# FNet mixing with a hard-swish MLP on one core: WN of two steps as products, an order of transfers, and tables that carry their zeros

## The chip, the cores and the metric

The kernel runs on one core of one Trainium2 chip. Its time is the device time of an execution in microseconds, the median of three runs. A profile of one more execution shows what each engine did: PE is the matmul engine (TensorE; PEld its weight loads), DVE is VectorE, ACT is ScalarE, POOL is GpSimd, SP is SyncE. SP only issues transfers here; ACT and POOL issue some beside their work.

## The reference

```python
# x: 8 x 3008 x 256, w_in: 256 x 2048, w_out: 2048 x 256, all float32
X = np.fft.fft(x, axis=1)
X = np.fft.fft(X, axis=2)
y = X.real.astype(np.float32).reshape(24064, 256)
h = y @ w_in
g = h * np.clip(h + 3.0, 0.0, 6.0) / 6.0
out = (g @ w_out).astype(np.float32)
```

## The kernel before

The transform along the sequence is split as 3008 = 47 x 64. The first stage is products with tables of 47 rows (`F`), the second stage products with tables of 64 rows per batch (`T`, six slices, one per group `gr` of four frequencies). The transform along the last axis is folded into w_in: `fold_w_in` multiplies a piece of w_in by the cosine and sine table `C` and writes `W1`. The batches are handled as four pairs; each pair has 12 chunks, and each chunk runs eight steps `fc` through the two MLP products. A step of a chunk is `mlp1_products` (u and v on PE), `activate` (VectorE adds, ACT relu, VectorE gates) and the products with w_out (`mlp2`, or `mlp2_first` in the first chunk).

All of this is steady from about 110 us on. Everything around the change is in the start. There the first pair is handled by halves (one batch at a time), and the first chunk's eight steps are interleaved by hand with the preparation of the weights, since each step needs its own piece of `W1` and `G` (the mixed w_out). The order of instructions on each engine is the order in which the program states them; no scheduler moves them.

The preparation of a weight piece `j` is: `load_w(j)` (a transfer that GpSimd issues), `exponent_a(j)` (ACT writes `PM`), `exponent_b(j)` (PE, `ex`), `exponent_c(j)` (ACT on `ex`), `mantissa(j)` (two VectorE instructions, L785 and L786), and `join(j)` (VectorE multiplies both; into `wi` for w_in, into `G` for w_out). For w_in, `fold_w_in(j)` follows: eight passes on PE (L827), a copy to `W1` (L830 or L834).

One row of the transformed input, the middle frequency, does not fit into the 127 rows that v has. It enters in `activate`: s = qn * WN + u (L566), with `qn` the row spread over all partitions, and `WN` the last row of W1's second block, turned into a column. Before, `send_wn` makes each of WN's 16 columns with a transfer from `W1[127, 1, f*128:(f+1)*128]` to `WN[:, f]` on SP's queue (L815), two after each fold.

First stage of batch 0: four units, in the order `FIRST`, each giving a tile `z`. `evict_first` copies it out of PSUM. Frequency groups 0 and 1 go from `z` to their place in `g` by direct transfers inside SBUF (`turn_first(gr, k)`, two per group and unit, L370); groups 2 and up go through DRAM later. Before, the loop issues both groups' transfers for each unit, and the last ones are placed by hand: one of group 0's last pair on ACT's queue, and group 1's last pair behind `fold_w_in(0)` with its two WN transfers. Group 0's `g` is multiplied by `stage2_half(hb, 0)` (L458) and `spread_by_pe` (L487) into `q` and `qn` for the first chunk; group 1's by a second `stage2_half` (L466) into `spare[0]`, copied to the second half of `q` (L1066).

Both of these take their table from `TF`, which comes with `c_dim`. `T` itself is used by all later second-stage products. For each batch b, 64 of its 128 rows hold the table and the other 64 must hold zeros. Before, `clear_table` writes the zeros with six memsets of 64 x 1024 on GpSimd (L888, at three places in `beside`), and `load_t` brings each slice in two transfers of 128 KB (L840).

SP and ACT share eight completion semaphores, used in turn; a transfer waits until the transfer that used its semaphore before has landed.

Of the kernel before, what the change touches and what calls it, by code (L numbers as in the profile page):

```python
# [7 lines left out]
F32 = mybir.dt.float32  # L8
# [41 lines left out]
N1, N2 = 47, 64  # L50
NK1 = (N1 + 1) // 2
# [7 lines left out]
def kernel(  # L59
# [10 lines left out]
    nc = tc.nc  # L70
    P = nc.NUM_PARTITIONS
# [12 lines left out]
    NM = NXC // 2  # L84
# [117 lines left out]
    def fold_columns(x, part, eng):  # L202
        near, far = x[:, :, 1:P], x[:, :, D - 1:P:-1]
        eng.tensor_tensor(near, near, far, op=AL.add)
        eng.scalar_tensor_tensor(far, far, (-2.0, 2.0)[part], near, op0=AL.mult, op1=(AL.add, AL.subtract)[part])
# [57 lines left out]
    def bank(shape, name):  # L263
        if starting[0]:
            return ps_a.tile(shape, F32, tag="acc", name=name)
        return ps_d.tile(shape, F32, tag="d", name=name)
# [100 lines left out]
    def turn_first(gr, k, last=nc.sync):  # L367
        for u in range(KK):
            to, fr = turns.pop((gr, k, u))
            (last if u else nc.sync).dma_start(out=to, in_=fr)  # L370
# [113 lines left out]
    def spread_by_pe(hb, ps, tab, copy=nc.scalar.copy):  # L484
        row_tile(first, 0)
        for u in range(KK):
            nc.tensor.matmul(ps[:, u * P:(u + 1) * P], hb.g[0][:, u, D:D + 1].to_broadcast([P, P]),  # L487
                             both_tables(0, 1, u, tab), start=True, stop=True)
        copy(first.qn[0][:, 0:TB], ps)
        del hb.g[0]  # L490
# [285 lines left out]
    def exponent_c(j):  # L776
        nc.scalar.activation(exs[j].bitcast(I32), exs[j], AF.Identity, scale=2.0 ** 23)
# [36 lines left out]
    def send_wn(f):  # L814
        nc.sync.dma_start(out=WN[:, f:f + 1], in_=W1[P - 1:P, 1, f * P:(f + 1) * P])  # L815

    def fold_w_in(j):

        _, n, k = PIECES[j]
        nb = WB // 2  # L820
        fc = 2 * n + k
        wi = w.pop(PIECES[j]).rearrange("p (i f) -> p i f", i=2)

        ps = bank([P, 2, nb], "wps") if starting[0] else spare[k]
        for blk in range(2):
            for i in range(2):
                nc.tensor.matmul(ps[:, blk], C[:, i, blk * P:(blk + 1) * P], wi[:, i], start=(i == 0), stop=(i == 1))  # L827
        if j == 1:
            for blk in range(2):
                nc.scalar.copy(W1[:, blk, fc * nb:(fc + 1) * nb], ps[:, blk])  # L830
                if blk == 0:
                    exponent_c(2)
        else:
            (nc.vector.tensor_copy if j == 0 else nc.scalar.copy)(W1[:, :, fc * nb:(fc + 1) * nb], ps[:])  # L834
        for f in range(2 * fc, 2 * fc + 2):
            send_wn(f)

    def load_t(gr, ks=slice(0, 2 * KK), queue=nc.sync):
        for b in range(2):
            queue.dma_start(out=T[b * N2:(b + 1) * N2, b, gr, :, ks], in_=c_stage2[gr, :, :, ks])  # L840


    def load_table():
# [21 lines left out]
    for i in range(2):  # L865
        nc.vector.memset(bias[:, i:i + 1], (2 * i - 1) * 7.5 / 16.0 - 896.0)
    E = FI[:, NIX + 1:].bitcast(F16).rearrange("p (i n) -> p i n", i=2)
    PM = [wpool.tile([P, 2, WB], I16, tag="PM", bufs=3, name="PM") for j in range(3)]

    def clear_bytes(j, eng=nc.vector):  # L870
        eng.memset(PM[j][:].rearrange("p i n -> p (i n)").bitcast(I32), 0x64006400)

# [3 lines left out]
    for k, t in enumerate(units[2:]):  # L876
# [3 lines left out]
        else:  # L880
            nc.scalar.copy(unused.rearrange("p (n d) -> p n d", n=2),
                           Z[PB // 2:PB].unsqueeze(1).to_broadcast([PB // 2, 2, 2 * TB]))

    def clear_table(b, groups, eng=None):
        r = slice((1 - b) * N2, (2 - b) * N2)
        t = T[r, b, groups].rearrange("p g a k n -> p g (a k n)")
        if eng:
            eng.memset(t, 0.0)  # L888
        else:
            nc.scalar.copy(t, Z[r].unsqueeze(1).to_broadcast([N2, groups.stop - groups.start, 2 * TB]))  # L890

    def head(j):
        exponent_a(j)
# [33 lines left out]
        hb.g[gr] = gpool.tile([P, 2 * KK, D + 1], F32, tag="g", name="g")  # L927
    for j in range(1, 3):
        clear_bytes(j, nc.gpsimd)
    fold_columns(zero.unsqueeze(1), 0, nc.vector)  # L930
    exponent_a(0)
    mantissa(0)
# [10 lines left out]
    for k, m in enumerate(FIRST):  # L943
        ps, pt = first_banks(m)
        x, xn = hb.x.pop(m), hb.xr.pop(m)
        unit_columns(m, 0, x, ps)
        if k > 0:
            evict_first(hb, FIRST[k - 1], *before)
            for gr in range(2 if k < NM - 1 else 1):
                turn_first(gr, k - 1)  # L950
        unit_middle(m, 0, x, pt)
        unit_middle(m, 1, xn, pt)
        for j in range(2) if k == NM - 1 else (None,):
            unit_columns(m, 1, xn, ps, j)
        before = ps, pt
    evict_first(hb, m, *before)
    turn_first(0, k, nc.scalar)
    turn_first(1, k - 1)

    seen = wpool.tile([P, 1], F32, tag="seen", name="seen")  # L960
    mantissa(1)
    fold_w_in(0)
    turn_first(1, k)
    exponent_a(1)
    keep_awake(1)
    exponent_b(1)
# [7 lines left out]
    mantissa(2)  # L974
    stage2_half(hb, 0, tab=TF)
    spread_by_pe(hb, bank([P, TB], "ps3")[:], TF)
    exponent_a(2)
    starting[0] = False
    spare = [ps_a.tile([P, 2, WB // 2], F32, tag="acc", name="spare") for h in range(2)]
# [5 lines left out]
    def beside(p):  # L985
        ahead, behind = {}, {}

        def put(t, f, *a, at=ahead):
            at.setdefault(t, []).append((f, a))

        cur = pairs[p]

        if p == 0:
            for gr in range(2, NG):
                put(gr, load_t, gr)
            for gr in range(2):
                put(14 + gr, load_t, gr)
            put(2, spread_half, halves[0], 1)
            for b in range(2):
                put(1, clear_table, b, slice(2, 4), nc.gpsimd)  # L1000
                put(2, clear_table, b, slice(4, NG), nc.gpsimd)
                put(9, clear_table, b, slice(0, 2), nc.gpsimd)
            put(4, load_table)
            put(NF - 1, close_w)
            for i, t in enumerate((3, 5, 7, 8)):
                put(t, mix_w_out, i)
            for gr in range(2, NSG):
                put(8 * gr - 10, load_g_half, halves[0], gr)
                put(8 * gr - 5, stage2_half, halves[0], gr)
                put(8 * gr - 4, spread_half, halves[0], gr)  # L1010

            hb = halves[1]
            put(1, load_zero, zero_slot(hb), hb, nc.sync)
            for k, m in enumerate(ORDER):
                if k > 0:
                    put((5, 8, 11)[k - 1], take_half, hb, m)
                    put((5, 8, 11)[k - 1], load_half, hb, m)
                for part in range(2):
                    put((4, 6, 11, 14)[k] + part, fold_half, hb, m, part, nc.gpsimd)
                put((8, 10, 15, 18)[k], stage1_quarters, hb, m, at=behind)  # L1020
            for gr in range(NSG):
                put(8 * gr + 23, load_g_half, hb, gr)
                put(8 * gr + 27 - (gr == 0), stage2_half, hb, gr)
                put(8 * gr + 28 - (gr == 0), spread_half, hb, gr)

        def s2(t, pr, gr):
            for i in range(2):
                put(t + 3 + 4 * i, stage2, pr, gr, i)
            put(t + 8, spread, pr, gr)

        for gr in range(1 if p > 0 else NSG, NG):
            if gr > 1:
                put(NST * (gr - 2) + 12, load_g, cur, gr)
            s2(NST * (gr - 1), cur, gr)
        if p + 1 < NP:
            nx = pairs[p + 1]
            for c in range(NXC):
                t = 9 * c if p > 0 else 24 + 6 * c
                put(t, load_x, nx, c)
                put(t + 3, fold, nx, c, 0, nc.gpsimd)  # L1040
                put(t + 5, fold, nx, c, 1, nc.gpsimd)
                put(t + 8, stage1, nx, c, at=behind)
            put(NST * (NG - 1) - 2, load_g, nx, 0)
            put(NST * (NG - 1) + 8, load_g, nx, 1)
            s2(NST * (NG - 1), nx, 0)
        return ahead, behind
# [15 lines left out]
    exponent_b(2)  # L1062
    activate(*chunk(0), *uv)
    ps = spare[0]
    stage2_half(halves[0], 1, copy=lambda o, i: None, ps=ps, tab=TF)
    nc.scalar.copy(first.q[0][:, :, TB:], ps[:])  # L1066
    mantissa(3)
    fold_w_in(1)
    join(2)
    exponent_a(3)  # L1070
    head(4)
# [109 lines left out]
def _tables(B, S, D):  # L1181
# [55 lines left out]
    for b in range(2):  # L1237
        rows = t[0:2, :, :, b::2].reshape(2, 2, 2, 4, 2, 2, 2, 2, N2)
        tf[:, b, :, :, :, :, :, :, :, b] = rows.transpose(4, 1, 2, 5, 3, 0, 6, 7, 8)
    d = np.concatenate([d.reshape(2, h, D).swapaxes(0, 1).reshape(h, -1), tf.reshape(h, -1)], axis=1)  # L1240
    return {
        "c_stage1": f.astype(np.float32),
        "c_stage2": t.astype(np.float32),
        "c_dim": d.astype(np.float32),
    }

# [30 lines left out]
```

## Time and profile before

| what | us |
|---|---|
| median of 3 runs (lowest, highest) | 1939.95 (1938.17, 1943.65) |
| the profiled execution | 1939.86 |
| its span | 1938.1 |
| PE busy | 1917.7 |
| VectorE busy | 1432.8 |
| GpSimd busy | 1449.7 |
| ACT busy | 677.4 |

The span begins and ends with the engines' instructions; the execution's time holds it and 1.76 us around it. In a row of the timeline stand the start, the length, the engine, the line, the operation, output<-input with shapes, how many, and in brackets the idle time ahead of it and what ended that. A row of the chain has start, length and what. "SPq" and "ACTq" are issues of transfers on those queues; the transfer itself goes on behind them.

### The profile page before, as it was taken

What the parts mean: (1) busy time and instruction counts of PE and PEld (TensorE: products, weight loads), DVE (VectorE), ACT (ScalarE), POOL (GpSimd) and SP (SyncE); (2) the same over time, 40 slices, a digit from 0 to 9 for tenths busy, and PEclk for the clock granted to TensorE, in tenths of its full rate; (3) what the DMA queues carried; (4) which work ended last, traced back from release to release, by engine and by line L of the source; (5) the groups of instructions that cost most, each with busy time, mean ns of one, the idle gap of its engine ahead of it and who ended that gap; (6) DMA issues with size and microseconds to landing.
All of it is one profiled execution on the core that took longest, in us unless ns stands there. A gap on an engine that the chain in (4) does not pass through costs nothing.

```text
span 1938.1 us, 28339 instructions
## 1 busy us (share of the span) xinstructions
PE 1917.7 (99%) x9398; PEld 1652.8 (85%) x9398; DVE 1432.8 (74%) x2754; ACT 677.4 (35%) x1166; POOL 1449.7 (75%) x1659
## 2 busy tenths in 40 slices
PE   8999999999999999999999999999999999999998
PEld 4578888888988888888898888888899888888888
DVE  7876776777777777777787777777778777777777
ACT  5533333333333333333333333333333333333332
POOL 4587888887678877787678887878667667666765
PEclk9999999999999999999999999999999999999999
DMA  7432122311111222111111221122110101101000
GB/s 252 122 96 55 51 73 69 82 44 32 38 34 50 61 72 55 44 50 32 37 36 47 56 55 44 50 52 53 36 28 20 28 17 26 31 17 28 17 21 20
DMA packets 154905, 98.21 MB, mean 51 GB/s; under 512 B 122319, under 2 KB 136378, under 8 KB 154758
## 3 DMA queue, kind: packets, MB, share of 16 engines
q1 hardware_dynamic: 142206, 57.58, 12.4%
q0 software_dynamic: 11264, 38.20, 6.7%
q8 instruction: 74, 1.21, 0.3%
q10 hardware_dynamic: 1288, 0.62, 0.1%
q14 instruction: 73, 0.60, 0.1%
HBM read 59.87 MB, written 36.79 MB: 50 GB/s over the span
## 4 chain that ended last, share of the span: by engine, by line
PE 95%; DVE 2%; DMA 1%; ACT 1%; issue 0%; ACTq 0%; SPq 0%; DVEq 0%
PE acc L652 56%; PE v L557 16%; PE u L557 16%; PE ps L505 2%; PE ps L277 1%; PE acc L632 1%; DVE a L608 1%; PE spare L827 1%; DVE s L566 0%; ACT t L605 0%; DMA WN<-W 0%; DVE o L713 0%; DMA g<-z 0%; DVE u L589 0%; PE ps L466 0%
## 5 line engine op out<-in xcount | busy, mean ns | idle before, releaser
L622 POOL TENSOR_TENSOR c<-a 128x512 f32<-128x512 f32 (+1 forms) x375 | 469.4, 1252 | 358.3 <-PE acc L652 301.5
L652 PE MATMUL acc<-c,G 128*128 128x256 f32 (+1 forms) x3008 | 697.2, 375 | 0.0
L605 ACT ACTIVATE t<-u,half 128x512 f32<-128x512 f32 (+1 forms) x384 | 260.6, 679 | 1146.3 <-DVE u L576 1067.0
L652 PEld LDWEIGHTS acc<-c,G 128*128 128x128 f32 x3008 | 565.2, 190 | 71.5 <-POOL c L622 0.4
L566 DVE SCALAR_TENSOR_TENSOR s<-qn,WN,u 128x256 f32<-128x256 f32 (+1 forms) x768 | 330.6, 472 | 344.2 <-PE u L557 338.3
L652 PE MATMUL acc<-a,G 128*128 128x256 f32 (+1 forms) x2256 | 541.6, 376 | 0.0
L652 PEld LDWEIGHTS acc<-a,G 128*128 128x128 f32 x2256 | 421.1, 189 | 73.6 <-issue 20.2
L557 PE MATMUL v<-q,W 127*128 127x256 f32 (+1 forms) x1536 | 389.5, 375 | 3.6 <-DVE a L608 3.6
L557 PE MATMUL u<-q,W 128*128 128x256 f32 (+1 forms) x1536 | 388.1, 375 | 0.5 <-ACT W L830 0.5
L608 DVE SCALAR_TENSOR_TENSOR a<-t,u 128x512 f32<-128x512 f32 (+2 forms) x448 | 264.2, 601 | 102.2 <-ACT t L605 97.5
L557 PEld LDWEIGHTS v<-q,W 127*128 127x128 f32 x1536 | 288.1, 190 | 44.0 <-DVE a L608 3.9
L557 PEld LDWEIGHTS u<-q,W 128*128 128x128 f32 x1536 | 285.8, 190 | 38.0 <-issue 2.6
L622 POOL TENSOR_TENSOR c<-a,c 128x256 f32<-128x256 f32 (+1 forms) x375 | 268.5, 716 | 29.4
L622 POOL TENSOR_TENSOR c<-c,a 128x256 f32<-128x256 f32 (+1 forms) x375 | 268.4, 716 | 29.4
L576 DVE TENSOR_TENSOR u<-s,v 128x512 f32<-128x512 f32 x352 | 245.0, 696 | 38.1 <-DVE s L566 1.9
L608 DVE SCALAR_TENSOR_TENSOR a<-t,v 128x512 f32<-128x512 f32 (+1 forms) x480 | 263.7, 566 | 0.3 <-ACT t L605 0.3
L605 ACT ACTIVATE t<-v,half 128x512 f32<-128x512 f32 (+1 forms) x384 | 260.5, 678 | 0.3 <-issue 0.3
L578 DVE TENSOR_TENSOR v<-v,s 128x512 f32<-128x512 f32 x352 | 243.9, 693 | 0.0
L622 POOL TENSOR_TENSOR r<-w,e 128x256 f32<-128x256 f32 (+1 forms) x92 | 88.7, 985 | 3.6
L662 ACT ACTIVATE e<-acc 128x512 f32<-128x512 f32 (+2 forms) x184 | 83.4, 544 | 0.0
L713 DVE STREAM_TRANSPOSE o<-r 128x256 f32<-128x256 f32 (+1 forms) x192 | 72.6, 415 | 0.2
L622 POOL TENSOR_TENSOR w<-w,e 128x512 f32<-128x512 f32 (+1 forms) x46 | 57.5, 1250 | 3.6
(127 smaller groups left out, 786.6 us busy)
## 6 DMA issues: line engine op xcount, KB each, us to landing
out_dram<-o SPq DMA_DIRECT2D x744, 32.0 KB
g<-zd SPq DMA_DIRECT2D x42, 256.0 KB
zd<-z SPq DMA_DIRECT2D x48, 192.0 KB
xt<-in_x_dram POOLq DMA_DIRECT2D x21, 256.0 KB, 3.7
st<-in_moe_w_out_dram POOLq DMA_DIRECT2D x8, 512.0 KB, 6.9
qn<-qd SPq DMA_DIRECT2D x16, 256.0 KB
st<-in_moe_w_in_dram POOLq DMA_DIRECT2D x7, 512.0 KB, 6.1
xt<-in_x_dram POOLq DMA_DIRECT2D x17, 192.0 KB, 4.1
```

The costliest lines, as they stand in the source:

```text
L277: nc.tensor.matmul(ps[b][h * PB:(h + 1) * PB, 0:n], F[rows(b), 0:PB], y[rows(b), 2 * h:2 * h + n], start=True, stop=not last, skip_group_c ...
L505: nc.tensor.matmul(ps[:, blk, u * P:n].rearrange("p (b k) -> p b k", b=2), g[:, kk, blk * (P + 1):blk * (P + 1) + P], T[:, :, gr, blk, kk, ...
L557: nc.tensor.matmul(ps[:, i, 0:nq], W1[r, blk, f * P:(f + 1) * P], q[r, blk, of:of + nq], start=True, stop=True)
L566: nc.vector.scalar_tensor_tensor(s[:, i, 0:nq], qn[:, of:of + nq], WN[:, f:f + 1], u[:, i, 0:nq], op0=AL.mult, op1=AL.add)
L576: nc.vector.tensor_tensor(u[:], s[:], v[:], op=AL.add)
L578: nc.vector.tensor_tensor(v[:], v[:], s[:], op=AL.subtract)
L605: nc.scalar.activation(t, h, AF.Relu, bias=half[:], scale=scale)
L608: nc.vector.scalar_tensor_tensor(dst, t, 1.0, h, op0=AL.min, op1=AL.mult)
L622: (eng or nc.gpsimd).tensor_tensor(out, in0, in1, op=AL.add)
L652: nc.tensor.matmul(ch.acc[i // 2][:, i % 2, 0:ch.n], G[:, i, fc, :], mv, start=(fc == 0 and i % 2 == 0), stop=(fc == NF - 1), skip_group_c ...
L662: nc.scalar.mul(ch.e[:, k:i + 1, 0:ch.n], ch.acc[i // 2][:, 0:i + 1 - k, 0:ch.n], 1.0 / WS)
L713: nc.vector.transpose(o[:, 0:n // DH, h], ch.r[:, m, h, 0:n].rearrange("p (j i) -> p j i", i=DH))
```

## The change

Three things change, all of them in the start or in what it prepares.

- WN of steps 0 and 1 (`fc` 0 and 1, four columns) comes from PE: `wn_by_pe(fc, ps)` multiplies each 128 x 128 block of `W1`'s second block by a unit column (`last_row`, a one in row 127, copied by GpSimd out of the identity that lies in `FI`), and VectorE copies the two results out of PSUM into `WN`. The WN transfers of these two steps go; those of steps 2 to 7 stay. Step 0's products stand behind `spread_by_pe`, step 1's behind the second `stage2_half`. With it, `fold_w_in(1)` moves ahead of that `stage2_half` on PE and its two copies ahead of q's copy on ACT.
- All of group 1's direct transfers are issued behind all of group 0's.
- The host's table `c_stage2` holds the zeros too, each slice with all 128 rows for both batches. `clear_table` goes, and `load_t` brings a slice in one transfer of 512 KB.

```diff
         if j == 1:
             for blk in range(2):
                 nc.scalar.copy(W1[:, blk, fc * nb:(fc + 1) * nb], ps[:, blk])
-                if blk == 0:
-                    exponent_c(2)
+            exponent_c(2)
...
-        for f in range(2 * fc, 2 * fc + 2):
-            send_wn(f)
-
-    def load_t(gr, ks=slice(0, 2 * KK), queue=nc.sync):
-        for b in range(2):
-            queue.dma_start(out=T[b * N2:(b + 1) * N2, b, gr, :, ks], in_=c_stage2[gr, :, :, ks])
+        if j > 1:
+            for f in range(2 * fc, 2 * fc + 2):
+                send_wn(f)
+
+    def wn_by_pe(fc, ps):
+        for i in range(2):
+            f = 2 * fc + i
+            nc.tensor.matmul(ps[:, i:i + 1], W1[:, 1, f * P:(f + 1) * P], last_row[:], start=True, stop=True)
+        nc.vector.tensor_copy(WN[:, 2 * fc:2 * fc + 2], ps)
+
+    def load_t(gr):
+        nc.sync.dma_start(out=T[:, :, gr].rearrange("p b a k n -> p b (a k n)"), in_=c_stage2[gr])
...
+    last_row = wpool.tile([P, 1], F32, tag="last_row", name="last_row")
...
-    def clear_table(b, groups, eng=None):
...
+    nc.gpsimd.tensor_copy(last_row[:], E[:, 0, P - 1:P])
...
             evict_first(hb, FIRST[k - 1], *before)
-            for gr in range(2 if k < NM - 1 else 1):
-                turn_first(gr, k - 1)
+            turn_first(0, k - 1)
...
     turn_first(0, k, nc.scalar)
-    turn_first(1, k - 1)
+    for i in range(NM):
+        turn_first(1, i)
...
     fold_w_in(0)
-    turn_first(1, k)
...
     spread_by_pe(hb, bank([P, TB], "ps3")[:], TF)
+    wn_by_pe(0, ps_d.tile([P, 2], F32, tag="d", name="wn")[:])
...
-            for b in range(2):
-                put(1, clear_table, b, slice(2, 4), nc.gpsimd)
-                put(2, clear_table, b, slice(4, NG), nc.gpsimd)
-                put(9, clear_table, b, slice(0, 2), nc.gpsimd)
...
     ps = spare[0]
+    fold_w_in(1)
     stage2_half(halves[0], 1, copy=lambda o, i: None, ps=ps, tab=TF)
     nc.scalar.copy(first.q[0][:, :, TB:], ps[:])
+    wn_by_pe(1, spare[1][:, 0, 0:2])
     mantissa(3)
-    fold_w_in(1)
     join(2)
```

More of the change, by code (lines that the diff above doesn't have):

```diff
@@ L882 @@
                            Z[PB // 2:PB].unsqueeze(1).to_broadcast([PB // 2, 2, 2 * TB]))
-    def clear_table(b, groups, eng=None):
[L885 to L890, printed above, removed]
     def head(j):
@@ L1239, in _tables @@
         tf[:, b, :, :, :, :, :, :, :, b] = rows.transpose(4, 1, 2, 5, 3, 0, 6, 7, 8)
+    ts = np.zeros((NK1 // 4, 2, N2, 2, 2, 4, N2))
+    for b in range(2):
+        ts[:, b, :, b] = t
     d = np.concatenate([d.reshape(2, h, D).swapaxes(0, 1).reshape(h, -1), tf.reshape(h, -1)], axis=1)
@@ L1242, in _tables @@
         "c_stage1": f.astype(np.float32),
-        "c_stage2": t.astype(np.float32),
+        "c_stage2": ts.reshape(NK1 // 4, 2 * N2, 2, -1).astype(np.float32),
         "c_dim": d.astype(np.float32),
```

## The prediction

> **What bounds the kernel now.** I read the page first: the span, the engines' shares and the chain that ended last.
>
> ```profile
> span 1938.1 us, 28339 instructions
> PE 1917.7 (99%) x9398; PEld 1652.8 (85%) x9398; DVE 1432.8 (74%) x2754; ACT 677.4 (35%) x1166; POOL 1449.7 (75%) x1659
> PE 95%; DVE 2%; DMA 1%; ACT 1%; issue 0%; ACTq 0%; SPq 0%; DVEq 0%
> ```
>
> PE carries 95% of the chain, and nothing that the change touches alters PE's steady work. What can be won lies in the other 5%, nearly all of it in the first 110 us. So I read the chain in order of time there (start, length, what).
>
> ```profile
> 14.67 6.95 DMA g<-z
> 21.72 1.18 ACTq L370
> 23.00 1.41 ACT PM L762 x2
> 24.44 0.38 PE ex L774
> 24.82 0.97 PE ps L458 x8
> 26.25 1.13 PE u L557 x4
> 29.57 1.74 PE spare L827 x8
> 33.10 7.08 DMA WN<-W
> 43.13 3.78 PE spare L827 x8
> 47.77 2.50 PE spare L827 x8
> 93.37 3.44 PE acc L632 x8
> ```
>
> Two transfers stand in the chain: a g<-z that ACT waits for, and the transfer that turns a row of W1 into a column of WN. The timeline shows the second one's price: VectorE waits 4.74 us for it, and PE stands still for 3.96 us behind it. Then I asked for the stretches (PE, PEld, DVE, ACT, POOL busy, granted clock, DMA share, GB/s).
>
> ```profile
> 38.94 0.48 DVE L566 SCALAR_TENSOR_TENSOR s<-qn,WN,u 128x256 f32<-128x256 f32 x1 [4.74 <-DMA WN<-W]
> 43.13 3.35 PE L827 MATMUL spare<-wi,C 128*128 128x256 f32 x7 [3.96 <-DVE wi L794]
> 40.00:42.00 2.00, 0.00 (x0) 0.00 (x0) 1.29 (x3) 0.07 (x1) 0.00 (x0) 1.00 1.03 403
> 44.00:46.00 2.00, 2.00 (x6) 1.53 (x6) 1.86 (x4) 1.02 (x2) 0.11 (x1) 0.50 0.00 0
> ```
>
> The stop costs twice: after it the granted clock is 0.50. The same eight products of L827 take 3.78 and 2.50 us there against 1.74 at 29.57. That is 2.0 + 0.8 us, and with the two ex products between them, about 3.2 us of slow PE behind 4 us of idle PE.
>
> **Part 1: the second group's transfers behind the first's.** In the order of the change, SP issues group 0's transfers for each z as it comes, and group 1's eight only behind all of them. ACT issues one of group 0's last two. Transfers of SP and ACT share eight completion semaphores in turn, and each waits for its semaphore's former user. ACT's transfer closes a row of twelve such transfers before and waits for one of the first four, which lands at 14.67 + 6.95 = 21.62. In the changed order it closes a row of eight, and its semaphore's former user is a constant's load from the start. So it waits only for z, which VectorE finishes last:
>
> ```profile
> 19.73 0.69 DVE L353 COPY z<-ps 128x512 f32<-128x512 f32 x1
> 22.20 0.59 SPq L370 DMA_DIRECT2D g<-z  x1
> ```
>
> That z is done at 20.42. The issue is then 20.46 to 21.64 at the same 1.18 us, the PM pair ends at 23.1 instead of 24.4, and the ex and group-0 products behind it follow: **-1.25 us**. Bounds: 0 if group 0's last transfers land later than 23.4; -1.8 if the issue takes the 0.6 us of most others. They should land in time: before, SP's last one of group 0 is the issue of 22.20 in the fence, over at 22.8, and the products begin at 24.82 without a wait for it, so it takes under 2 us.
>
> Group 1's eight issues follow at about 0.62 us each from 21.1, so the last ends near 26.1 (26.7 before, where two WN transfers stood in between). The cover for this delay is the fold of W1's second step, which now comes ahead of group 1's products on PE: 1.74 us.
>
> **Part 2: WN of steps 0 and 1 by products.** Each wn_by_pe is two f32 matmuls with one moving column, four weight loads in all. Eight passes of 128 columns at L458 take 0.97 us, 0.12 each. No row shows 128-wide weights with a single moving column. If the load sets the pace, four passes take 0.45 us; if the moving side does, nearly nothing. I take 0.45, since those passes are load and product in equal parts, and keep 0.1 to 0.5. VectorE's copy of 128x2 out of PSUM: between the 0.06 us of a tiny instruction and 0.2; I take 0.15. GpSimd's copy of the unit column is one tiny instruction beside its waits: nothing. The four WN transfers removed free 2.4 us of SP's queue, which nobody waits for.
>
> Step 0 did not wait for WN; its s had waited 0.27 us for PE:
>
> ```profile
> 27.49 0.87 DVE L566 SCALAR_TENSOR_TENSOR s<-qn,WN,u 128x256 f32<-128x256 f32 x2 [0.27 <-PE u L557]
> ```
>
> So there the product only costs, **+0.45 us**, since u waits behind it on PE. With part 1, step 0 runs 0.8 us earlier.
>
> Step 1. ACT's order is now: t, t, both W1 copies, ex, then q.
>
> ```profile
> 30.44 0.58 ACT L1066 COPY q<-spare 128x512 f32<-128x512 f32 x1
> 31.33 0.37 ACT L830 COPY W<-spare 128x256 f32<-128x256 f32 x1 [0.31 <-PE spare L827]
> 31.60 0.59 ACT L777 ACTIVATE ex<-ex 128x512 int32<-128x512 f32 x1
> 31.76 1.13 PE L557 MATMUL u<-q,W 128*128 128x256 f32 x4 [0.46 <-ACT W L830]
> 36.37 1.07 ACT L777 ACTIVATE ex<-ex 128x512 int32<-128x512 f32 x2 [1.25 <-PE ex L774]
> 37.34 1.40 ACT L762 ACTIVATE PM<-st,bias 128x512 uint8<-128x512 int16 x2
> ```
>
> q began at 30.44 behind t; with the 0.85 us lead the first W1 copy begins at 29.6. The steps between starts here (0.27, 0.27, 0.52, then 0.6 for q) put q's end at 31.25 and u at 31.3, against 31.76. The second wn_by_pe (30.4 to 30.85) lies inside that wait of PE: nothing. The WN transfer is gone, so what is late next? VectorE could start s at 34.1: behind WN's copy at 31.1 stand two mantissa pairs (1.15 each) and a join (0.7). PE, from u at 31.3: u 0.86, v 0.86, acc 1.72, four ex products 0.86, to 35.6. ACT: two ex 1.07 and the PM pair 1.40, to 38.15; only then t, and VectorE's gate of step 1 at 38.95 instead of 42.99. So the stall of 4.74 us is not won whole; ACT's queue becomes the limit: **-4.05 us** there, parts 1 and 2 together.
>
> Behind it VectorE works almost without gap, except in two places:
>
> ```profile
> 44.19 0.42 DVE L785 TENSOR_SCALAR top<-st 128x512 int32<-128x512 int32 x1
> 46.67 2.12 POOL L888 MEMSET T<- 64x1024 f32 x2
> 46.71 1.19 DVE L785 TENSOR_SCALAR top<-st 128x512 int32<-128x512 int32 x1
> 53.06 0.75 DVE L800 TENSOR_TENSOR G<-top,spare 128x256 f32<-128x256 f32 x2 [1.45 <-ACT spare L777]
> ```
>
> The 1.45 us is a wait for an ex that PE made late at half clock. Without the stop PE keeps its clock, does the first fold from 38.6 to 40.3, and is 6.5 us ahead by then: the wait goes, **-1.45 us**. **Part 3** starts here: the memsets of T on GpSimd go, and the mask instruction that ran beside one (1.19 us against 0.42) gets its 0.77 us back: **-0.8 us**. Sum at 53 us: -4.05 - 1.45 - 0.8 = -6.3 us, PE's lead (-6.5) just above it, so VectorE sets it.
>
> On the clock: the Trainium skill (TensorE: Matmul & The Clock Gate, on why this matters for kernels) says that PE idle beyond some 3 us between bursts brings half rate back. The first stop agrees (3.96 us, then 0.50). The next one does not quite:
>
> ```profile
> 75.88 1.50 PE L557 MATMUL v<-q,W 127*128 127x256 f32 x4 [2.79 <-DVE a L608]
> 77.38 4.76 PE acc L632 x8
> 76.00:78.00 2.00, 2.00 (x5) 1.28 (x6) 2.00 (x5) 2.00 (x4) 1.64 (x6) 0.62 0.31 46
> ```
>
> 2.79 us were enough here. So I count a stop of 2.8 us with its clock loss (v 0.64 and acc 4.76 - 3.44 = 1.32 longer, 1.96 us); by the page's 3 us alone this stop would be free of it, and nothing of it could be won.
>
> **Part 3, the rest.** That stop is VectorE's: its mask and fraction instructions run slowly while GpSimd mixes G and folds x.
>
> ```profile
> 59.92 1.95 POOL L888 MEMSET T<- 64x1024 f32 x2
> 68.00 1.04 DVE L785 TENSOR_SCALAR top<-st 128x512 int32<-128x512 int32 x1
> 69.07 1.10 DVE L786 SCALAR_TENSOR_TENSOR top<-st,top 128x512 f32<-128x512 uint32 x1
> ```
>
> Without the 1.95 us of memset ahead of it, GpSimd's work is done 2 us sooner against VectorE's order, so the last slow pair (1.04 and 1.10 against 0.42 and 0.69) may run free: **-1.0 us**. Bounds: 0, if GpSimd's work meets other instructions as slow; -4, if the stop falls by 2 us and its clock loss goes too. I take -1.0. The third pair of memsets, on GpSimd in the steady part, lies beside products that PE has anyway: 0.
>
> Each T slice now brings its zeros: 512 KB in one transfer instead of 256 KB in two. At 403 GB/s, 256 KB are 0.65 us, for each of six slices, four of them during the start. The products of the start read TF, not T, and SP saves an issue per slice. What stands behind the first slice on SP is the qd and qn pair and the WN transfers of steps 4 and 5:
>
> ```profile
> 65.12 2.47 SPq L815 DMA_DIRECT2D WN<-W  x4
> ```
>
> They are used just ahead of the stop at 73, 5 us after the last issue, and they wait for ACT's W1 copy as much as for the slice. I price the slices at nothing; 0.65 us if that margin is gone.
>
> **The sum.** 1939.86 us is the profiled execution's own time (1.8 us outside its span), 0.1 from the median 1939.95. -6.3 - 1.0 = -7.3: **1932.6 us**. 0.3% is 5.8 us, about what a measurement of this kernel can tell from no change.
>
> **Rivals.**
>
> *The second stop goes as well.* If VectorE gains 2 us before 72 us, PE waits under 1 us and keeps its clock: -6.3 - 2 - 1.96 = -10.3, 1929.6 us. For it: the slow pairs stand just ahead of the stop. Against: GpSimd has as much other work.
>
> *The early lead is lost.* If group 0 lands late or ACT's issue is no earlier, -1.25 falls out, and the last -1.0 may: -5.05, 1934.8 us, within the bound. For it: four short waits in a row must all follow.
>
> *Group 1 lands late; slower.* Now ACT's q copy and VectorE's WN copy both stand behind group 1's products, with four PM and two mantissa pairs queued behind them, so lateness counts one for one. GpSimd's weight loads are issued at 25.2 instead of 26.5, and under their load a transfer took 7.08 us:
>
> ```profile
> 26.49 0.72 POOL L755 DMA_DIRECT2D st<-in_moe_w_out_dram  x1
> 28.00:29.00 1.00, 1.00 (x9) 0.77 (x7) 0.90 (x2) 0.00 (x0) 1.00 (x2) 1.00 0.83 147
> ```
>
> The loads' data move 1.5 us behind the first issue (DMA share 0.83 from 28), so from 26.7 in the changed kernel, when group 1's last transfer has just been issued. It is needed at 29.6. It decides from there: landing at 33 (7 us, as WN's did), PE stops 3.6 us and drops its clock, and only 0.5 to 1 us is left of the gain, 1939 us. Behind the whole backlog, which drains near 42, it would land about 40: u of step 1 at 41.5, ten later than before, the gate at 49.2, +6.2 us: 1946 us. Against it: only one load is ahead of it in any order. The Trainium skill (DMA: Bandwidth & Descriptors, on queues and rings) says that each DMA engine takes turns between queues; by that the wait would be under a microsecond. The 7.08 us of WN's 512 bytes disagree, so I keep the chance.
>
> **How the numbers follow.** Forecast 0.40; second stop gone 0.20; early lead lost 0.22; group 1 late but not slower 0.10; slower 0.08. Faster by over 0.3%: 0.60; within it 0.32; slower by over it 0.08. The range leaves out the last two cases: from 1929.0 (the second stop with its bound) to 1937.0 (the lead lost and half of one more term).
>
> **What would show it.** Right: ACT's L370 issue near 20.5; u of step 1 near 31.3; s without a wait for a DMA; the gate of step 1 near 39, behind ACT's PM; clock 1.00 from 42 to 50; G<-top,spare at about 46.7 without a wait. Wrong: PE waiting at L466 for g, a granted clock below 1 before 60, or everything up to 75 early by 6 us and the lead given back later, which none of these terms allows.

## The result and the profile after

| | median us | lowest, highest | span of the profiled execution |
|---|---|---|---|
| before (6 runs) | 1940.58 | 1938.17, 1943.65 | 1938.1 |
| after (6 runs) | 1931.52 | 1929.91, 1935.19 | 1929.2 |

The ratio is 0.9954, with an interval of 0.9941 to 0.9967: about 9 us faster, where 7.3 were forecast. The profiled spans differ by 8.9 us. The page of the kernel after, the three parts that were shown of before:

```profile
span 1929.2 us, 28340 instructions
PE 1914.9 (99%) x9406; PEld 1652.3 (86%) x9406; DVE 1429.9 (74%) x2756; ACT 677.7 (35%) x1166; POOL 1444.9 (75%) x1654
PE 95%; DVE 2%; ACT 1%; POOL 1%; DMA 0%; issue 0%; ACTq 0%; DVEq 0%; SPq 0%; POOLq 0%
```

PE's share of the chain is the same 95%. The 1% of DMA is gone. Everything that was won lies ahead of the first product of the second half (L381). That product starts at 105.68 before and at 96.66 after, 9.02 us earlier, and what remains of the span behind it is 1832.4 and 1832.5 us. The timeline of before has two rows that the start of after is compared with, the gate of step 1 and that product:

```profile
42.99 0.68 DVE L608 SCALAR_TENSOR_TENSOR a<-t,u 128x512 f32<-128x512 f32 x1
105.68 1.08 PE L381 MATMUL ps<-y,F 47*64 47x512 f32 x8
```

The timeline of after, from the last z to the gate of step 1:

```profile
20.19 0.69 DVE L353 COPY z<-ps 128x512 f32<-128x512 f32 x1 [0.69 <-PE ps L342]
20.96 1.43 ACTq L370 DMA_DIRECT2D g<-z  x1
22.49 1.39 ACT L762 ACTIVATE PM<-st,bias 128x512 uint8<-128x512 int16 x2 [1.85 <-DMA g<-z]
24.25 1.13 PE L458 MATMUL ps<-TF,g 128*128 128x128 f32 x8
26.63 0.15 DVE L842 COPY WN<-wn 128x2 f32<-128x2 f32 x1
30.00 1.30 PE L466 MATMUL spare<-TF,g 128*128 128x128 f32 x8
31.50 1.11 PE L557 MATMUL u<-q,W 128*128 128x256 f32 x4
34.72 0.86 DVE L566 SCALAR_TENSOR_TENSOR s<-qn,WN,u 128x256 f32<-128x256 f32 x2
37.21 1.40 ACT L762 ACTIVATE PM<-st,bias 128x512 uint8<-128x512 int16 x2
39.22 0.69 DVE L608 SCALAR_TENSOR_TENSOR a<-t,u 128x512 f32<-128x512 f32 x1 [1.65 <-ACT t L605]
```

ACT's issue now follows z by 0.08 us (before, z ended at 20.42 and the issue came at 21.72). s of step 1 has no wait in brackets, where 4.74 us for the WN transfer stood. The gate waits for ACT, as forecast; ACT's PM pair ends at 38.61 (forecast 38.15, with a z that came 0.46 later).

Where the two stops stood, the timeline of after has:

```profile
38.88 1.89 PE L827 MATMUL spare<-wi,C 128*128 128x256 f32 x8
42.41 1.99 PE L827 MATMUL spare<-wi,C 128*128 128x256 f32 x8 [0.40 <-DVE wi L794]
47.21 0.75 DVE L800 TENSOR_TENSOR G<-top,spare 128x256 f32<-128x256 f32 x2
67.94 1.13 PE L557 MATMUL v<-q,W 127*128 127x256 f32 x4 [0.70 <-DVE a L608]
```

The stretches there (PE, PEld, DVE, ACT, POOL busy, granted clock, DMA share, GB/s):

```profile
44.00:46.00 2.00, 2.00 (x7) 0.90 (x7) 1.86 (x6) 0.59 (x1) 0.00 (x0) 1.00 0.66 217
70.00:72.00 2.00, 2.00 (x6) 0.84 (x5) 1.82 (x4) 0.78 (x2) 1.72 (x5) 1.00 0.32 48
```

And the chain, the step behind v and the transfer that the end of this section speaks of:

```profile
69.07 3.44 PE acc L632 x8
75.99 4.42 DMA WN<-W
```

The fold that stood 3.96 us for wi now starts at 38.88 without such a wait (the next one waits 0.40 us), and the clock stays at 1.00; G<-top,spare starts at 47.21 without its wait of 1.45. The stop of 2.79 us ahead of v is 0.70, its clock loss is gone too, and acc takes 3.44 us instead of 4.76.

A new wait stands behind it, for the WN transfer of step 6 (the chain's 75.99). The timeline's rows:

```profile
80.44 0.48 DVE L566 SCALAR_TENSOR_TENSOR s<-qn,WN,u 128x256 f32<-128x256 f32 x1 [0.51 <-DMA WN<-W]
96.66 1.08 PE L381 MATMUL ps<-y,F 47*64 47x512 f32 x8
```

### The profile page after: what moved, and what is told of

It is laid out like the page before. It is cut to its first block, busy times and chain, and to the rows that moved or that the text cites. A ratio compares the mean times of both kernels' runs of the same rounds, so it can differ in the third digit from the quotient of the medians.

```text
span 1929.2 us, 28340 instructions
## 1 busy us (share of the span) xinstructions
PE 1914.9 (99%) x9406; PEld 1652.3 (86%) x9406; DVE 1429.9 (74%) x2756; ACT 677.7 (35%) x1166; POOL 1444.9 (75%) x1654
## 4 chain that ended last, share of the span: by engine, by line
PE 95%; DVE 2%; ACT 1%; POOL 1%; DMA 0%; issue 0%; ACTq 0%; DVEq 0%; SPq 0%; POOLq 0%
PE acc L652 56%; PE v L557 16%; PE u L557 16%; PE ps L505 2%; PE ps L277 1%; PE acc L632 1%; DVE a L608 1%; PE ps L342 0%; ACT t L605 0%; DVE s L566 0%; PE spare L827 0%; POOL c L622 0%; DVE o L713 0%; ACT PM L762 0%; PE ps L466 0%
```

## The experiments

The theory was the prediction's account, with the second stop now counted in. WN by products removes the first stop. The memsets on GpSimd make the second one, by slowing VectorE's mask and fraction instructions. The order pays only with the other parts. The rivals were that the clock loss carries most of the gain, that the order does nothing, and that the second stop goes because the start is faster. Each kernel was timed side by side with the kernel before: eleven executions in the first table, five or six in the others. A time "to L381" is the start of that product in the profile, before 105.68.

### Each part alone

WN by products, with the fold ahead; order and tables as before:

```diff
-        for f in range(2 * fc, 2 * fc + 2):
-            send_wn(f)
+        if j > 1:
+            for f in range(2 * fc, 2 * fc + 2):
+                send_wn(f)
...
+    wn_by_pe(0, ps_d.tile([P, 2], F32, tag="d", name="wn")[:])
...
+    fold_w_in(1)
...
+    wn_by_pe(1, spare[1][:, 0, 0:2])
...
-    fold_w_in(1)
```

> Only the products for WN of steps 0 and 1, with the fold of step 1 moved ahead as in the change; transfers and memsets as before. Theory (the first stop and its slow clock are the products' work, the second stop hangs on GpSimd's memsets): the first stop goes, G<-top,spare of step 1 begins about 5.0 us earlier than 53.06, but PE still waits some 2.8 us for a of step 4 and drops its clock there; total about -5 us against before. Rival (the second stop goes by itself once the first is gone, the memsets play no part): about -9 us.

The tables with their zeros, without `clear_table`; the rest as before:

```diff
-        for b in range(2):
-            queue.dma_start(out=T[b * N2:(b + 1) * N2, b, gr, :, ks], in_=c_stage2[gr, :, :, ks])
...
+        nc.sync.dma_start(out=T[:, :, gr].rearrange("p b a k n -> p b (a k n)"), in_=c_stage2[gr])
...
-            for b in range(2):
-                put(1, clear_table, b, slice(2, 4), nc.gpsimd)
-                put(2, clear_table, b, slice(4, NG), nc.gpsimd)
-                put(9, clear_table, b, slice(0, 2), nc.gpsimd)
```

> Only the table slices with their zeros, no memsets; WN and the group transfers as before. Theory: the first stop of 4 us and its half clock stay as they are, VectorE is about 2 us ahead by the second stop, PE waits under 1 us there and keeps its clock: 2.1 + 1.7, about -3.8 us. Rival (the memsets play no part, 1.5 MB more of transfers cost something): 0 to +1 us.

The order of the transfers; the rest as before:

```diff
-            for gr in range(2 if k < NM - 1 else 1):
-                turn_first(gr, k - 1)
+            turn_first(0, k - 1)
...
-    turn_first(1, k - 1)
+    for i in range(NM):
+        turn_first(1, i)
...
     fold_w_in(0)
-    turn_first(1, k)
```

> Only group 1's transfers behind all of group 0's; WN by transfers for all steps, the fold of step 1 where it was. Theory: WN of step 0 now stands behind group 1's eight issues and lands about 1 us after it is wanted, and group 1's products come ahead of the fold and wait about 2 us for their last transfers; the group-0 products start only 0.4 us earlier: +1 to +2 us. By the prediction's own first term (a lead of 1.25 us that is passed on): -1 us.

Nothing of the change, but nine more products in PE's first stop, whose results are not used:

```diff
+            for i in range(9):
+                nc.tensor.matmul(spare[0][:, 0], ones[:], W1[:, 0, 0:TB], start=True, stop=True)
```

> The kernel before, with nine products of 0.43 us on PE whose result nobody reads, put where PE waits for wi behind the WN transfer (39.2 to 43.1). The wait of VectorE for WN stays; only PE's idleness goes. Theory (the stop costs twice, by idling and by the clock behind it): the clock stays 1.00 from 42 to 50, the folds take 1.74 us instead of 3.78 and 2.50, G<-top,spare no longer waits its 1.45 us for the ex, and the time falls by about 1.5 us; more than that cannot come, since VectorE sets the pace behind. Rival (PE's clock loss is hidden behind VectorE anyway): 0.

| kernel | median us (before: 1940.95) | ratio [interval] | to L381 |
|---|---|---|---|
| products only | 1937.38 | 0.9979 [0.9970, 0.9988] | 101.73 |
| tables only | 1937.22 | 0.9982 [0.9973, 0.9991] | 102.25 |
| order only | 1941.82 | 1.0009 [1.0000, 1.0018] | 107.60 |
| PE kept busy | 1940.20 | 0.9997 [0.9988, 1.0006] | 104.98 |

The profile of the products alone begins late: its last z is ready at 22.36, against 20.42 before. So its time to L381 understates what it wins. From the end of the last z to L381 it takes 79.37 us with the products only and 81.28 with the tables only, against 85.26 before and 75.78 after.

The timeline at the second stop, of the kernel with the products only:

```profile
71.92 1.47 PE L557 MATMUL v<-q,W 127*128 127x256 f32 x4 [2.79 <-DVE a L608]
```

The stretch:

```profile
72.00:74.00 2.00, 2.00 (x5) 1.30 (x6) 2.00 (x4) 2.00 (x4) 1.65 (x7) 0.64 0.31 46
```

And of the kernel with the tables only, from the first stop on:

```profile
44.58 3.26 PE L827 MATMUL spare<-wi,C 128*128 128x256 f32 x8 [3.95 <-DVE wi L794]
73.96 1.13 PE L557 MATMUL v<-q,W 127*128 127x256 f32 x4 [0.71 <-DVE a L608]
85.64 0.87 DVE L566 SCALAR_TENSOR_TENSOR s<-qn,WN,u 128x256 f32<-128x256 f32 x2 [1.34 <-DMA WN<-W]
```

The stretch:

```profile
74.00:76.00 2.00, 2.00 (x7) 1.39 (x8) 2.00 (x4) 2.00 (x4) 1.93 (x5) 1.00 0.70 245
```

The two parts take one stop each. With the products the first stop is gone and the second is still 2.79 us, clock loss included. With the tables the first is still 3.95 us and the second is 0.71, at a clock of 1.00. So the second stop hangs on GpSimd's memsets, not on how early the start is done. The wait for WN of step 6 appears here with the tables (1.34 us).

The order alone won nothing. The timeline of that kernel has SP's issues, PE's wait within group 1's products, and VectorE's s of step 0:

```profile
26.71 12.76 SPq L815 DMA_DIRECT2D WN<-W  x4
30.56 0.89 PE L466 MATMUL spare<-TF,g 128*128 128x128 f32 x4 [2.04 <-issue]
31.90 0.48 DVE L566 SCALAR_TENSOR_TENSOR s<-qn,WN,u 128x256 f32<-128x256 f32 x1 [5.39 <-DMA WN<-W]
```

The WN transfers of steps 0 and 1 now stand behind group 1's eight on the same queue, and step 0, which did not wait for WN before, waits 5.39 us, where about 1 us was expected. PE waits 2.04 us between the two halves of group 1's products, about what was expected. The order needs WN by products.

With PE kept busy the first stop's clock loss goes, and VectorE's wait stays; its timeline:

```profile
40.20 0.48 DVE L566 SCALAR_TENSOR_TENSOR s<-qn,WN,u 128x256 f32<-128x256 f32 x1 [5.34 <-DMA WN<-W]
```

The stretch:

```profile
44.00:46.00 2.00, 1.60 (x7) 1.44 (x8) 1.97 (x5) 2.00 (x4) 0.00 (x0) 1.00 0.02 4
```

The clock is 1.00, and the product at L381 comes 0.70 us earlier, or 1.36 us counted from L458, which starts 0.66 us later in this profile. The time's interval holds no change and allows 2.3 us. So by the profile the first stop's clock loss carries about a microsecond, which the times don't tell from nothing; most of the stop's price is VectorE's wait itself.

### One part taken back

The change with the memsets and the half slices as before:

```diff
-        nc.sync.dma_start(out=T[:, :, gr].rearrange("p b a k n -> p b (a k n)"), in_=c_stage2[gr])
+        for b in range(2):
+            queue.dma_start(out=T[b * N2:(b + 1) * N2, b, gr, :, ks], in_=c_stage2[gr, :, :, ks])
...
+            for b in range(2):
+                put(1, clear_table, b, slice(2, 4), nc.gpsimd)
+                put(2, clear_table, b, slice(4, NG), nc.gpsimd)
+                put(9, clear_table, b, slice(0, 2), nc.gpsimd)
```

> The change with the memsets and the half slices of before put back: products for WN and the order of the group transfers alone. Theory (the second stop hangs on the memsets): PE waits 2.8 us for a of step 4, drops its clock, total -4.5 us against before. Rival (the second stop is only an echo of the first): -9 us.

The change with both groups' transfers issued unit by unit as before:

```diff
-            turn_first(0, k - 1)
+            for gr in range(2 if k < NM - 1 else 1):
+                turn_first(gr, k - 1)
...
-    for i in range(NM):
-        turn_first(1, i)
+    turn_first(1, k - 1)
...
     fold_w_in(0)
+    turn_first(1, k)
```

> The change with both groups' transfers issued together for each unit, as before. Theory (the order's lead is 0.4 us at the group-0 products, and 0.2 to 0.3 us of it goes again in waiting for group 1): the same as the whole change within 1 us, -8 to -9 us. By the prediction's first term (-1.25 us, passed on whole): -7.8 us.

| kernel | median us (before: 1940.93) | ratio [interval] | to L381 |
|---|---|---|---|
| without tables | 1934.86 | 0.9965 [0.9952, 0.9979] | 100.95 |
| without order | 1933.49 | 0.9964 [0.9952, 0.9976] | 98.96 |

Without the tables the stop is back. The timeline of that kernel:

```profile
55.54 1.95 POOL L895 MEMSET T<- 64x1024 f32 x2
71.13 1.13 PE L557 MATMUL v<-q,W 127*128 127x256 f32 x4 [2.79 <-DVE a L608]
```

The stretch:

```profile
72.00:74.00 2.00, 2.00 (x5) 0.93 (x4) 1.90 (x5) 1.32 (x2) 1.64 (x4) 0.56 0.30 46
```

The time alone (6 to 7 us faster than before) lies between what the two theories gave; the rows decide. What the tables are worth in the whole change is 2.1 us by the ratios, whose intervals overlap, and 4.3 in the profiles to L381 (of which 0.84 is a wait of PE at L466 in this profile). The five times of this kernel spread from 1932.43 to 1935.81, and the profiled one, 1935.38, is among the slower; so the stop itself is shown, its price in the time only roughly.

Without the order the ACT issue is late again, and the timeline at the start reads:

```profile
22.94 1.18 ACTq L370 DMA_DIRECT2D g<-z  x1
25.02 0.38 PE L774 MATMUL ex<-PM,FI 128*128 128x512 f16 x1 [1.91 <-ACT PM L762]
26.05 1.91 PE L458 MATMUL ps<-TF,g 128*128 128x128 f32 x8
```

The stretch:

```profile
26.00:28.00 2.00, 2.00 (x11) 2.00 (x11) 1.06 (x3) 0.96 (x3) 0.34 (x2) 0.50 0.18 48
```

z was ready at 21.09 here, and the issue came 1.85 us behind it (0.08 in after). PE waits 1.91 us and its clock drops. I had expected the order to be worth at most 0.4 us, reading it from the one profile of after; the medians differ by 2.0 and the ratios by 0.0010, and from the end of the last z to L381 it takes 77.87 us here, 2.09 more than after. The intervals overlap, so its size is not settled. The direction is that of the forecast's first term, 1.25.

### Moving what is left

The change with four slices of T loaded at steps 2, 9, 12 and 13 instead of 2 to 5, run twice:

```diff
-                put(gr, load_t, gr)
+                put((2, 9, 12, 13)[gr - 2], load_t, gr)
```

> The whole change, with the last three table slices loaded at steps 9, 12 and 13 instead of 3, 4 and 5, out of the way of WN's transfers. Theory (behind the two stops the next wait is WN of step 6, 0.51 us on VectorE and 0.37 on PE): that wait goes, -0.4 us against the whole change, about -9.4 us against before; no wait for WN at s of step 6 in the trace. Rival (the slices are hidden): -9.0 us.

> The change with the late slices once more, on the same chip as the changed kernel: 0.7 us less than the changed kernel by its first trace (96.00 - 20.96 against 96.66 - 20.88 from the last z to the first product of the second half), which is near what a measurement can tell.

The change with half slices, and all six memsets later, where PE was thought to cover them:

```diff
-        nc.sync.dma_start(out=T[:, :, gr].rearrange("p b a k n -> p b (a k n)"), in_=c_stage2[gr])
+        for b in range(2):
+            queue.dma_start(out=T[b * N2:(b + 1) * N2, b, gr, :, ks], in_=c_stage2[gr, :, :, ks])
...
+            for b in range(2):
+                put(8, clear_table, b, slice(2, 4), nc.gpsimd)
+                put(9, clear_table, b, slice(4, NG), nc.gpsimd)
+                put(9, clear_table, b, slice(0, 2), nc.gpsimd)
```

> The whole change, but with zeros written by GpSimd after all, all six memsets at steps 8 and 9, and the half slices of before. Theory (what counts is that GpSimd's queue is free between 45 and 65 us, not where the zeros come from): the second stop stays short, -9 us. Rival (the memsets delay GpSimd's c just as the steady products begin, which wait for it): 2 to 6 us of it are lost.

The later slices, and GpSimd's first fold of the second half one step later, run twice:

```diff
-                put(gr, load_t, gr)
+                put((2, 9, 12, 13)[gr - 2], load_t, gr)
...
-                    put((4, 6, 11, 14)[k] + part, fold_half, hb, m, part, nc.gpsimd)
+                    put((5, 6, 11, 14)[k] + part * (k > 0), fold_half, hb, m, part, nc.gpsimd)
```

> The change with the late slices, and GpSimd's first fold of the second half moved from step 4 to step 5, behind its wait for PE. Theory (VectorE's mask and fraction instructions are slow only while GpSimd works beside them): the pairs of pieces 10 and 11, 0.87 + 1.24 + 0.87 in the changed kernel, fall to 0.42 + 0.69 + 0.42, and PE's last 0.7 us of waiting for a of step 4 goes: 0.7 us less than with the late slices alone. Rival (GpSimd's later folds then meet later pairs, or hold the gathers back): nothing, or 1 us lost.

> The late slices and the later fold once more, for a profile in which the first gathers of x land as in the others (there the last z was ready at 25.7 instead of 20.3 to 21.5 us). Theory: from the first group-0 product to the first product of the second half 70.6 us as there, against 71.7 to 72.4 with the change and with late slices; span about 1928, time -10 us against before. Rival (the 70.6 us came from the late start, which gave the weights time to arrive): 71.7 us, -9 us.

The change itself, beside them:

> The changed kernel itself once more, beside the two versions built on it: -9 us against before, as on its first measurement.

| kernel | median us (before) | ratio [interval] | to L381 |
|---|---|---|---|
| slices later | 1931.23 (1940.93) | 0.9961 [0.9947, 0.9974] | 96.00 |
| slices later, again | 1932.26 (1941.31) | 0.9956 [0.9942, 0.9969] | 96.76 |
| zeros late | 1932.66 (1940.93) | 0.9964 [0.9951, 0.9978] | 96.50 |
| folds later | 1930.69 (1941.31) | 0.9947 [0.9933, 0.9961] | 100.59 |
| folds later, again | 1929.38 (1940.79) | 0.9942 [0.9928, 0.9956] | 96.81 |
| the change again | 1931.31 (1941.31) | 0.9951 [0.9937, 0.9964] | 96.31 |

Moving the slices takes step 6's wait for WN away in all four runs that have it, and with half slices at the old steps (zeros late) it does not come either: so the slices of 512 KB at these steps bring that wait. They don't always: without the order they stood there too, and step 6 did not wait. The wait is 0.51 us in one profile of the change and 0.22 in the other. From v of step 4 to L381 these two take 28.72 and 28.43 us, and both runs with the slices later 28.12. The times don't resolve it: the expected 0.4 us is not seen in them (0.9961 and 0.9956, against 0.9954 and 0.9951 of the change).

With the zeros late the second stop stays short (0.70), as the theory has it, and 1.9 us are lost later, as the rival has it: the span behind L381 is 1834.4 us instead of 1832.5. The timeline of GpSimd there shows four memsets between instructions that make `c`:

```profile
104.94 0.73 POOL L622 TENSOR_TENSOR c<-a,c 128x256 f32<-128x256 f32 x1
105.72 3.73 POOL L895 MEMSET T<- 64x1024 f32 x4
109.42 1.27 POOL L622 TENSOR_TENSOR c<-a 128x512 f32<-128x512 f32 x1
```

GpSimd's work on the steady path is delayed by 3.73 us there. That this is where the 1.9 us go was not tried by itself.

With the fold later PE no longer waits at the second stop at all in either run. In the change that fold (L216 and L217) begins at 57.16, beside two pairs of VectorE's mask and fraction instructions. In the second run it begins at 68.82, and the first three instructions of these pairs are:

```profile
59.28 0.60 DVE L785 TENSOR_SCALAR top<-st 128x512 int32<-128x512 int32 x1
59.91 0.69 DVE L786 SCALAR_TENSOR_TENSOR top<-st,top 128x512 f32<-128x512 uint32 x1
61.38 0.42 DVE L785 TENSOR_SCALAR top<-st 128x512 int32<-128x512 int32 x1
```

In after they took 0.87, 1.24 and 0.87 us; here they take 0.60, 0.69 and 0.42, as the theory has it but for 0.18 us of the first. The second run is the fastest kernel measured, 0.9942 against 0.9951 of the change, but the intervals overlap. From the first group-0 product to L381 it took 72.37 us, more than either expectation had (70.6 and 71.7). In that profile PE lost 1.12 us at the start:

```profile
32.11 0.68 PE L466 MATMUL spare<-TF,g 128*128 128x128 f32 x4 [1.12 <-issue]
```

So both runs of that version come out no slower than the change; that it beats it is not shown.

## Why the prediction was right

The range held the time, and 1932.6 lies 1.1 us above the median. Part of that closeness is luck: the forecast starts from one execution of before, 1939.86, which lies 0.7 us below the median of its six. The change won 9.1 us by the medians where 7.3 were forecast. What happened, then, is the rival *the second stop goes as well* (1929.6), less what other terms fell short of it. Step by step, from the profiles:

| step | forecast | measured |
|---|---|---|
| part 1, to the end of the PM pair | -1.25 | -0.97 counted from z's end (the issue took 1.43 us instead of 1.18), -0.5 counted from the start of the span, since z came 0.46 later |
| WN of step 0 by products | 0.45 on PE | 0.34 in the chain |
| VectorE's copy of WN | 0.15 | 0.15 |
| gate of step 1 | -4.05, behind ACT's PM | -3.77, behind ACT's PM |
| G<-top,spare at 53 us | -6.3 | -5.85 |
| the rest of part 3, VectorE | -1.0 | -2.1 to the second stop |
| the same stop's clock loss | 0 | -1.7 |
| slices of T | 0 | +0.6 behind WN of step 6 |
| sum | -7.3 | -9.05 |

The first four rows lie within the fifth, and the sum counts from the fifth on. Counted from z's end, the gate of step 1 is 4.23 us earlier and G<-top,spare 6.31, as forecast (4.05 and 6.3). The signs that the prediction named for being right came in: s of step 1 waits for no DMA, its gate waits for ACT, the clock is 1.00 from 42 to 50, and G<-top,spare has no wait. So the prediction's mechanism held up to 53 us, and what it missed lies behind.

The measured terms from 53 us on are differences of starts: v goes from 75.88 to 67.94 (-7.94, so 2.1 more than the 5.85), and acc's end from 82.14 to 72.51 (-9.63, another 1.7).

**The mis-sized term** is part 3's rest. The prediction freed one slow pair of mask and fraction instructions. The timeline of after shows VectorE's and GpSimd's rows ahead of the second stop:

```profile
57.56 0.87 DVE L785 TENSOR_SCALAR top<-st 128x512 int32<-128x512 int32 x1
58.47 1.24 DVE L786 SCALAR_TENSOR_TENSOR top<-st,top 128x512 f32<-128x512 uint32 x1
61.99 0.42 DVE L785 TENSOR_SCALAR top<-st 128x512 int32<-128x512 int32 x1
62.44 0.69 DVE L786 SCALAR_TENSOR_TENSOR top<-st,top 128x512 f32<-128x512 uint32 x1
64.80 0.73 POOL L810 TENSOR_TENSOR G<-G 128x256 f32<-128x256 f32 x1 [3.74 <-PE acc L632]
```

GpSimd runs out of work at 61.1 and stands until 64.80. The two pairs of VectorE in that time (61.99 to 64.9) run at 0.42 and 0.69 us each, against 0.87 and 1.24 for a pair beside a busy GpSimd. Over the four pairs ahead of the stop that is 5.89 us instead of 7.94, which is the 2.1 us. The kernel with the fold later bears this out: with GpSimd's fold moved away the slow pairs run nearly free. The argument against the rival, that GpSimd has as much other work, failed: GpSimd was not behind any more, but ahead, waiting for PE. The Trainium skill (GPSIMD Engine Reference, key points) says that GpSimd shares its SBUF interfaces with VectorE, with contention for VectorE instructions that run in a 2-port mode or have two SBUF inputs. These rows agree for L786, which reads `st` and `top`; whether L785 runs in such a mode no run here shows.

**The slices** were priced at nothing because of a margin of 5 us at steps 4 and 5. Those steps did not wait. Step 6, which the prediction did not look at, did. The price named for a lost margin, 0.65 us, is near the 0.61 of this profile by chance: in the change's second profile it is 0.31.

**The rivals.** *The early lead is lost* did not happen. *Group 1 lands late* was only grazed: L466's eight passes took 1.30 us in after (1.05 in the change's second profile). PE waited 0.84 us ahead of the second half of them without the tables, and 1.12 us in the second run with the folds later; the profile names no releaser for these two waits. The stop that the prediction reckoned with was 3.6 us.

## What to carry to other kernels

A transfer in a chain of short steps can be replaced by a small product when PE stands still there anyway: four one-column passes at 0.34 us took the place of a transfer of 7.08. Before an idle engine's work is priced at nothing, ask which other engine's instructions run beside it: memsets of 1.95 us on GpSimd shifted its later work onto VectorE's, and cost 3.8 us, by the profiles, at a stop 13 us later; the times show less, 2.1 us without the tables and 3.5 with the tables only, with wide intervals. Parts of a change can depend on each other: the order alone made step 0 wait 5.39 us for WN, a wait that the products take away.

## What the runs showed of the hardware

PE's granted clock dropped after shorter waits than 3 us. Waits of 0.70 to 1.14 us left it at 1.00 (0.70 in after, 1.12 above, 1.14 before at 23.80). After every stop of 2.79 us it was 0.50 to 0.56 in the slowest two-microsecond stretch behind it (before, products only, order only, PE kept busy, without tables). It also fell to 0.50 after 1.91 us without the order, after 2.04 us with the order only, and after 1.43 us at the start of the products only. The 1.60 us ahead of the very first product left it at 1.00. The timeline and a stretch of the products only:

```profile
20.89 0.71 PE L342 MATMUL ps<-xt,F 47*64 47x129 f32 x13 [1.43 <-issue]
22.00:24.00 2.00, 2.00 (x6) 1.55 (x6) 1.39 (x3) 0.21 (x1) 0.00 (x0) 0.50 0.21 63
```

The stretch behind the wait of 2.04 us with the order only:

```profile
32.00:34.00 2.00, 2.00 (x6) 1.55 (x6) 0.38 (x1) 0.00 (x0) 1.04 (x2) 0.50 1.04 363
```

The Trainium skill (TensorE: Matmul & The Clock Gate, why this matters for your kernels) puts the bound at some 3 us between bursts; these rows put it lower here. No run changed the length of a wait alone, so where the bound lies is not shown, nor whether the wait alone decides.

In the first profile of the folds-later kernel the clock was low with PE busy all the time, as a stretch of it shows.

```profile
20.00:22.00 2.00, 2.00 (x27) 1.68 (x23) 0.00 (x0) 1.07 (x2) 0.00 (x0) 0.50 0.56 216
```

The timeline:

```profile
25.02 0.69 DVE L353 COPY z<-ps 128x512 f32<-128x512 f32 x1 [5.66 <-PE ps L342]
```

Its last z came 4.8 us later than that of after, and VectorE had waited 5.66 us for PE's products. So the late z goes with the slow PE; the expectation of the second run had put it down to the gathers of x. Why the clock was low there is open. That execution was the slowest of its five (1934.87 against a median of 1930.69). So part of the spread between runs arises ahead of the last z, and a step of a microsecond is better read from z's end than from the span's start.

ACT's issue of a transfer took 1.42 to 1.43 us right behind z, beside SP's issues, and 1.18 to 1.24 where it came later. The cause was not tried.
